# Attention and two gated feed-forward layers: in later batches VectorE's maxima and low parts stand behind an inverse

## The chip, the cores and the metric

One core of one Trainium2 chip runs the whole kernel. The metric is the device time of one execution in microseconds (us), less is better.

## What is computed

Attention over 4 batches of 8 heads, 576 positions, 64 columns a head; its output is one matrix of 2304 tokens x 512, which goes through two feed-forward layers. Heads 0 to 3 see a local window of 32 positions, heads 4 to 7 the positions at a distance that 32 divides.

```python
scores = scale * np.matmul(q, k.transpose(0, 1, 3, 2))
mask_local = (rel >= 0) & (rel < stride)          # stride = 32
mask_strided = (rel >= 0) & (pos[None, :] % stride == pos[:, None] % stride)
scores = np.where(masks[None, :, :, :], scores, -1000000000.0)
scores = scores - np.max(scores, axis=-1, keepdims=True)
attn = np.exp(scores)
attn = attn / (np.sum(attn, axis=-1, keepdims=True) + 1e-09)
out = np.matmul(attn, v)
x = out.transpose(0, 2, 1, 3).reshape(2304, 512)
xn = x / np.sqrt(np.mean(x * x, axis=-1, keepdims=True) + 1e-06) * rms_g
g = xn @ w_gate                                   # 512 x 1536
x = (g * (1.0 / (1.0 + np.exp(-g))) * (xn @ w_val)) @ w_out
```

The second layer is the last two lines again, with weights of its own and without the norm. All is float32.

## The kernel before

**Products.** A float32 matrix is held as a high part, rounded to the type that TensorE multiplies at full speed (fp32r), and a low part, what is left. A product is three matmuls: high by high, high by low, low by high. ScalarE casts the high part (L305 of a weight, L1000 of the tokens), VectorE subtracts it from the float32 source and so gets the low part (`lo`, L309, of a weight; L1001 in `split`, of the tokens). The gate's weights come by DMA into `raw` and `dh` buffers, are scaled (L288 and its neighbours), and split.

**Attention.** Each of the four batches has ten groups: five of strided heads and then five of local heads. A group goes through steps. `softmax_step` (L663): TensorE makes the scores in a PSUM bank; `top` has VectorE add the mask and take the negative maximum of each row, one instruction a head (L677, into `e` and `nb`; a program's listing shows a second row behind each, for the column `nb`); `exp` has ScalarE take the exponential and the row sums (L686); `norm` has VectorE add 1e-9 to the sums (L696) and take the inverse (L697, `rc`), and GpSimd multiply the weights by it (L703). `turn_step` (L712): TensorE transposes the weights into a bank (L80), and ScalarE (L87) or VectorE (L89) copies the bank to SBUF. A last step multiplies by V; its output is copied into `x` in SBUF and stored. Transposes of Q and K (`qn`, to `qT` and `kT`) go the same way, through L80 and L87 or L89. After the first batch five banks (a0, a1, y1, y2, y3) go round among these steps. A transpose or product that writes a bank has to wait until the bank's last reader is done.

**Feed-forward in between.** While attention runs, the first layer already works on the tokens that are ready, in segments of 256 or 512 tokens (the first at token 0, then 256, 512, 1024, 1536 and 1792). For each of twelve column blocks of 128 it makes the gate product (`gate`, bank `b_g`), the silu of it (L977, L978, `sg`), the value product (bank `b_v`), their product (L985), that one's high and low parts (L988 and L989, `hh` and `hl`), and the product with `w_out` (`down`). Between these, calls of `point()` let the attention steps go on by one phase: so TensorE's work alternates. The scheduler orders each engine's queue by a priority of each instruction; the feed-forward's own pieces have a higher one (`ahead`). After all attention, from about 206 us on, the remaining work is a long run of feed-forward passes that combine blocks so that seven products do for eight; these fill the rest of the span.

**Tokens.** `split` (L998) makes the high and low parts of a segment's tokens, for each of four column chunks. `here` (L1005) calls it for what attention has just left in SBUF. `split_x` (L1015) calls it for the columns that attention wrote to DRAM earlier: `load_x` has them loaded into `xraw`, two tiles, each with a single buffer that the next segment's load fills again. SyncE issues that load at L160.

**Order.** An instruction can be put behind another on the same engine without a wait: `tc.issue_after` sets an edge that only the order of issue keeps. The kernel uses it like this:

```python
    def behind(eng):
        return tc.issue_after(last[eng]) if eng in last else nullcontext()
```

`last["dve"]` and `last["act"]` hold VectorE's and ScalarE's latest `top`, `exp`, `silu` or `hidden` instruction, and `lo` stands behind `last["dve"]`. The functions that the diff touches follow, with the profile's line numbers.

Of the kernel before, what the change touches and what calls it, by code (L numbers as in the profile page):

```python
# [8 lines left out]
F32 = mybir.dt.float32  # L9
# [3 lines left out]
ALU = mybir.AluOpType  # L13
# [12 lines left out]
def attn_ffn_ffn(ctx: ExitStack, tc: tile.TileContext, q, k, v, w1g, w1v, w1o, rms_g, w2g, w2v, w2o, out):  # L26
    nc = tc.nc
# [65 lines left out]
    last = {}  # L93
# [211 lines left out]
            nc.scalar.copy(out=t[:, 0], in_=src)  # L305

    def lo(t, src):
        with behind("dve"):
            nc.vector.tensor_tensor(out=t[:, 1], in0=src, in1=t[:, 0].bitcast(F32), op=ALU.subtract)  # L309

    def weight_step(m, c, z, park=False):
# [11 lines left out]
        def second():  # L323
            lo(cell["t"], cell["h"])
            spent(cell["bk"], 4)
            wt[m, c, z] = cell["t"]
            wdone.add((m, c, z))
# [154 lines left out]
    def behind(eng):  # L482

        return tc.issue_after(last[eng]) if eng in last else nullcontext()
# [10 lines left out]
    class Attention:  # L495
# [167 lines left out]
        def softmax_step(self, ready, key, qn, kn, mks, mms):  # L663

            cell = {}
            nt = len(mks)

            def pe():
                cell["s"] = mms()

            def top():
                sp = cell["s"]
                cell["e"] = e = self.p2.tile([128, 4, 128], F32, tag="e", name="e", bufs=6)
                cell["nb"] = nb = self.p2.tile([128, 32], F32, tag="nb", name="nb", bufs=6)
                for i, mk in sorted(enumerate(mks), key=lambda im: im[0] % 2):

                    r = nc.vector.tensor_tensor_reduce(out=e[:qn, i, :kn], in0=sp[i], in1=mk[:qn, :kn], scale=-0.125,  # L677
                                                       scalar=3.0e38, op0=ALU.add, op1=ALU.min, accum_out=nb[:qn, i:i + 1])
                if state["start"]:
                    last["dve"] = ins_of(r)  # L680

            def exp():
                e, nb = cell["e"], cell["nb"]
                cell["sums"] = sums = self.p2.tile([128, 32], F32, tag="sums", name="sums", bufs=6)
                for i in range(nt):
                    r = nc.scalar.activation(out=e[:qn, i, :kn], in_=e[:qn, i, :kn], func=AF.Exp, bias=nb[:qn, i:i + 1],  # L686
                                             scale=-1.0, accum_out=sums[:qn, i:i + 1])
                if state["start"]:
                    last["act"] = ins_of(r)

            def norm():
                e, sums = cell["e"], cell["sums"]
                rc = self.p2.tile([128, 32], F32, tag="rc", name="rc", bufs=6)
                self.nnorm = getattr(self, "nnorm", -1) + 1
                eng = nc.gpsimd
                nc.vector.tensor_scalar(out=sums[:qn, :nt], in0=sums[:qn, :nt], scalar1=1e-9, scalar2=None, op0=ALU.add)  # L696
                nc.vector.reciprocal(out=rc[:qn, :nt], in_=sums[:qn, :nt])  # L697
                if eng is None:
                    for i in range(nt):
                        nc.vector.tensor_scalar(out=e[:qn, i, :kn], in0=e[:qn, i, :kn], scalar1=rc[:qn, i:i + 1], scalar2=None,  # L700
                                                op0=ALU.mult)
                if eng is not None:
                    eng.tensor_tensor(out=e[:qn, :nt, :kn], in0=e[:qn, :nt, :kn], in1=rc[:qn, :nt].unsqueeze(2).to_broadcast([qn, nt, kn]), op=ALU.mult)  # L703
                if key[1] == 0 or not 3:
                    self.st[key] = e

            def put():
                self.st[key] = cell["e"]

            return Step([pe, top, exp, norm] + ([wait] * (3 - 1) + [put] if 3 and key[1] else []), ready, kind="s")  # L710

        def turn_step(self, key, qn, kn, nt):  # L712
# [223 lines left out]
    def pieces(parts, t0, n):  # L936

        for a, w, d in parts:
            lo, hi = max(a, t0), min(a + w, t0 + n)
            if lo < hi:  # L940
                yield lo - t0, lo - a, hi - lo, d
# [28 lines left out]
    def ins_of(r):  # L970
        return getattr(r, "ins", r)
# [19 lines left out]
    def x_tiles(si):  # L991
        if si not in tiles_of:
            p, w = pools[si % 2]
            tiles_of[si] = [tuple(p.tile([128, w], F32R, tag=f"x{z}{c}", name="x" + z) for z in "hl") for c in range(KC)]
        return tiles_of[si]

    @ahead
    def split(si, o, w, src):  # L998
        for c, (xh, xl) in enumerate(x_tiles(si)):
            ra = nc.scalar.copy(out=xh[:, o:o + w], in_=src(c))  # L1000
            rd = nc.vector.tensor_tensor(out=xl[:, o:o + w], in0=src(c), in1=xh[:, o:o + w].bitcast(F32), op=ALU.subtract)  # L1001
            if si == 0:
                last["act"], last["dve"] = ins_of(ra), ins_of(rd)

    def here(b, o, w):  # L1005

        lo, hi = b * S + o, b * S + o + w
        for si in range(1, min(cur[0] + 2, NA)):
            t0, n = segs[si][1:3]
            a, e = max(lo, t0), min(hi, t0 + n)  # L1010
            if a < e:
                have_to.setdefault(si, set()).add((lo, hi))
                split(si, a - t0, e - a, lambda c: att.x[b, c // 2][:, c % 2, a - b * S:e - b * S])

    def split_x(si):  # L1015
        t0, n = segs[si][1:3]
        if si in xraw:
            x0, x1, todo = xraw.pop(si)
            for lo, hi in todo:
                a, e = max(lo, t0), min(hi, t0 + n)  # L1020
                split(si, a - t0, e - a, lambda c: (x0, x1)[c // 2][:, c % 2, a - t0:e - t0])
        return tiles_of[si]
# [122 lines left out]
    with tc.high_priority(offset=PRIO_R):  # L1145
        split(0, 0, early[0][1], lambda c: att.x[0, c // 2][:, c % 2, :early[0][1]])
        xs_of = {0: tiles_of[0]}
# [443 lines left out]
    for n, (m, cs, t0) in enumerate(work):  # L1591
# [88 lines left out]
        c = chunks[-1]  # L1680
# [47 lines left out]
```

## Time and profile before

| | |
|---|---|
| three runs | 993.5, 998.85, 996.44 us (median 996.44) |
| the profiled execution | 994.36 us |
| its span | 992.5 us, 17794 instructions |
| mean granted TensorE clock | 0.997 of full speed |
| TensorE busy | 968.8 us, 98% of the span |
| VectorE busy | 578.1 us, 58% |
| ScalarE busy | 577.9 us, 58% |
| GpSimd busy | 388.1 us, 39% |

The time of an execution is the span, from its first to its last instruction, and 1.9 us around it (994.36 - 992.5). The profile was taken of one execution, so its rows add up to its span and not to the median. The granted clock is that of TensorE: 1.00 is 2.4 GHz, and the lower of its two levels, 1.2 GHz, reads as 0.50; a mean between them is a stretch that has both. "Idle before" in brackets is the time in which the engine did nothing just before an instruction, with what ended it; "issue" there means that the profile shows nothing that it waited for.

### The profile page before, as it was taken

The page shows a single profiled execution, that of the slowest core. Times are in us where ns is not written, and L with a number is a line of the kernel's source. Part 1 is how long each engine was busy: PE and PEld are TensorE (multiplying, and loading weights), DVE is VectorE, ACT ScalarE, POOL GpSimd, SP SyncE. Part 2 cuts the span into 40 slices and gives each one's busy share as a digit, 9 for nine tenths or more (in the row PEclk, how much of TensorE's full clock was granted, in tenths as well). Part 3 has the DMA queues.
Part 4 walks back from the last instruction along what each step waited for, and adds up shares of the span by engine and source line. Part 5 has one row for each costly group of instructions (what it writes and reads, how often), then busy time and mean ns, then how long its engine had stood idle before and what let it go on. Part 6 is the DMA issues. An engine that isn't in the chain of part 4 may idle for free.

```text
span 992.5 us, 17794 instructions
## 1 busy us (share of the span) xinstructions
PE 968.8 (98%) x6054; PEld 892.0 (90%) x6054; DVE 578.1 (58%) x1319; ACT 577.9 (58%) x1465; POOL 388.1 (39%) x416
## 2 busy tenths in 40 slices
PE   8889999999999999999999999999999999999998
PEld 8778877778989999999999998999999999989997
DVE  5786777856436556466656646545557554653334
ACT  6988686855545555556564546555666546553431
POOL 3221252641321637343534646471615344341500
PEclk9989999999999999999999999999999999999999
DMA  7884648829994756995759685466888396864311
GB/s 197 230 218 147 162 153 260 261 90 303 307 319 151 219 173 224 323 321 174 251 175 325 220 279 209 155 221 241 310 269 267 114 342 220 289 206 161 97 53 64
DMA packets 168455, 215.89 MB, mean 218 GB/s; under 512 B 46860, under 2 KB 122028, under 8 KB 168364
## 3 DMA queue, kind: packets, MB, share of 16 engines
q1 hardware_dynamic: 158559, 199.48, 62.4%
q10 hardware_dynamic: 9805, 15.27, 4.3%
q8 instruction: 48, 0.79, 0.3%
q14 instruction: 43, 0.35, 0.1%
HBM read 142.87 MB, written 71.83 MB: 216 GB/s over the span
## 4 chain that ended last, share of the span: by engine, by line
PE 84%; ACT 6%; DMA 5%; DVE 3%; issue 1%; POOL 1%; SPq 0%; DVEq 0%; POOLq 0%; ACTq 0%
PE b_y L76 36%; PE b_a L76 17%; PE b_g L76 14%; PE b_v L76 13%; PE b_y L80 2%; ACT e L686 2%; DMA raw<-in_moe_w_out_dram 1%; PE b_a L80 1%; DMA pk<-dh 1%; ACT raw L288 1%; PE b_v L72 1%; ACT dh L280 1%; DMA pk<-raw 1%; DVE dh L297 1%; DMA ob<-part 1%
## 5 line engine op out<-in xcount | busy, mean ns | idle before, releaser
L1401 POOL TENSOR_TENSOR xl<-xst,xh 128x384 fp32r<-128x384 f32 x196 | 211.8, 1102 | 178.9 <-ACT xh L1400 60.1
L76 PE MATMUL b_y<-xh,w 128*128 128x384 f32 (+1 forms) x800 | 215.6, 335 | 1.4 <-ACT t L1458 1.1
L76 PEld LDWEIGHTS b_y<-xh,w 128*128 128x128 f32 x800 | 145.9, 188 | 4.4 <-ACT t L1458 1.7
L76 PE MATMUL b_a<-xh,w 128*128 128x384 f32 (+2 forms) x512 | 141.3, 335 | 1.8 <-ACT t L1458 1.6
L76 PE MATMUL b_y<-xl,w 128*128 128x384 f32 (+1 forms) x400 | 133.8, 334 | 0.0
L76 PE MATMUL b_g<-xh,w 128*128 128x384 f32 (+2 forms) x408 | 125.6, 348 | 0.1
L76 PE MATMUL b_v<-xh,w 128*128 128x384 f32 (+2 forms) x344 | 104.6, 347 | 1.4 <-ACT t L1472 1.4
L76 PEld LDWEIGHTS b_a<-xh,w 128*128 128x128 f32 x512 | 93.2, 188 | 5.4 <-ACT t L1458 3.1
L386 POOL TENSOR_TENSOR raw<-dh 128x256 f32<-128x256 f32 x40 | 29.6, 758 | 160.6 <-DVE dh L297 69.0
L1400 ACT CAST xh<-xst 128x384 fp32r<-128x384 f32 x196 | 91.5, 520 | 0.0
L76 PE MATMUL b_a<-xl,w 128*128 128x384 f32 (+2 forms) x256 | 85.8, 335 | 0.0
L76 PE MATMUL b_y<-hh,w 128*128 128x384 f32 (+2 forms) x304 | 81.2, 341 | 0.0
L76 PEld LDWEIGHTS b_g<-xh,w 128*128 128x128 f32 x408 | 75.6, 190 | 5.5 <-issue 0.5
L76 PEld LDWEIGHTS b_y<-xl,w 128*128 128x128 f32 x400 | 75.2, 188 | 1.8
L76 PE MATMUL b_g<-xl,w 128*128 128x384 f32 (+2 forms) x204 | 69.1, 339 | 0.0
L76 PEld LDWEIGHTS b_v<-xh,w 128*128 128x128 f32 x344 | 62.9, 188 | 6.5 <-ACT t L1472 1.7
L703 POOL TENSOR_TENSOR e<-e,rc 128x384 f32<-128x384 f32 (+3 forms) x40 | 37.0, 929 | 79.3 <-DVE nb L677 17.0
L76 PE MATMUL b_y<-w,hh 128*128 128x512 f32 x216 | 67.1, 391 | 0.0
L686 ACT ACTIVATE e<-e,nb 128x96 f32<-128x96 f32 (+2 forms) x152 | 56.7, 377 | 5.0 <-DVE nb L677 5.0
L76 PE MATMUL b_v<-xl,w 128*128 128x384 f32 (+2 forms) x172 | 58.0, 337 | 0.0
L76 PEld LDWEIGHTS b_y<-hh,w 128*128 128x128 f32 x304 | 54.8, 188 | 3.1 <-issue 0.2
L1478 DVE TENSOR_TENSOR b_y<-b_y,t 128x384 f32<-128x384 f32 x56 | 31.7, 566 | 41.7 <-ACT b_y L1472 40.8
(216 smaller groups left out, 2150.8 us busy)
## 6 DMA issues: line engine op xcount, KB each, us to landing
w<-pk SPq DMA_DIRECT2D x48, 512.0 KB
raw<-in_moe_w_gate_dram SPq DMA_DIRECT2D x24, 512.0 KB
raw<-in_moe_w_val_dram SPq DMA_DIRECT2D x24, 512.0 KB
raw<-in_moe_w_out_dram SPq DMA_DIRECT2D x24, 512.0 KB
pk<-raw ACTq DMA_DIRECT2D x48, 256.0 KB
part<-ob SPq DMA_DIRECT2D x48, 256.0 KB
xst<-y_d SPq DMA_DIRECT2D x30, 384.0 KB
xst<-xq SPq DMA_DIRECT2D x28, 384.0 KB
```

What stands on the lines that cost most here:

```text
L72: traced(nc.tensor.matmul(att.fill, att.warm[:, :128], att.warm, start=True, stop=True))
L76: traced(nc.tensor.matmul(out_, a, b_, start=start, stop=stop, **how))
L80: traced(nc.tensor.transpose(out_, a, one))
L280: nc.scalar.activation(out=cell["h"], in_=cell["hw"].bitcast(F32), func=AF.Copy, scale=2.0 ** -112)
L288: nc.scalar.activation(out=cell["r"], in_=cell["lw"], func=AF.Copy, scale=LOW)
L297: nc.vector.scalar_tensor_tensor(out=h, in0=h, scalar=3, in1=cell["r"], op0=ALU.logical_shift_left, op1=ALU.bitwise_or)
L386: paced(nc.gpsimd.tensor_tensor(out=t[:, z], in0=a, in1=b, op=ALU.subtract))
L686: r = nc.scalar.activation(out=e[:qn, i, :kn], in_=e[:qn, i, :kn], func=AF.Exp, bias=nb[:qn, i:i + 1], scale=-1.0, accum_out=sums[:qn, i:i ...
L703: eng.tensor_tensor(out=e[:qn, :nt, :kn], in0=e[:qn, :nt, :kn], in1=rc[:qn, :nt].unsqueeze(2).to_broadcast([qn, nt, kn]), op=ALU.mult)
L1400: nc.scalar.copy(out=xh[:, kk], in_=src[:, kk])
L1401: paced(nc.gpsimd.tensor_tensor(out=xl[:, kk], in0=src[:, kk], in1=xh[:, kk].bitcast(F32), op=ALU.subtract), ("pe", None))
L1478: nc.vector.tensor_tensor(out=s, in0=s, in1=v, op=ALU.mult)
```

## The change

Every inverse of row sums that `norm` makes is noted as `last["sum"]`, if the second part of the group's key is not 0; that is so in batches 1 to 3 and not in batch 0. Three kinds of VectorE instructions then stand behind the inverse noted last: the maxima of `top`, the low parts of weights in `lo`, and the low parts of tokens in `split`. "Noted last" goes by the order in which the program is written down: whatever is written after an inverse comes behind it in VectorE's queue. No instruction is added or taken away, and none changes its size. Until the first inverse of batch 1 is noted, nothing is different.

```diff
--- before.py
+++ after.py
@@ -305,7 +305,7 @@
             nc.scalar.copy(out=t[:, 0], in_=src)
 
     def lo(t, src):
-        with behind("dve"):
+        with behind("dve"), behind("sum"):
             nc.vector.tensor_tensor(out=t[:, 1], in0=src, in1=t[:, 0].bitcast(F32), op=ALU.subtract)
 
     def weight_step(m, c, z, park=False):
@@ -674,8 +674,9 @@
                 cell["nb"] = nb = self.p2.tile([128, 32], F32, tag="nb", name="nb", bufs=6)
                 for i, mk in sorted(enumerate(mks), key=lambda im: im[0] % 2):
 
-                    r = nc.vector.tensor_tensor_reduce(out=e[:qn, i, :kn], in0=sp[i], in1=mk[:qn, :kn], scale=-0.125,
-                                                       scalar=3.0e38, op0=ALU.add, op1=ALU.min, accum_out=nb[:qn, i:i + 1])
+                    with behind("sum"):
+                        r = nc.vector.tensor_tensor_reduce(out=e[:qn, i, :kn], in0=sp[i], in1=mk[:qn, :kn], scale=-0.125,
+                                                           scalar=3.0e38, op0=ALU.add, op1=ALU.min, accum_out=nb[:qn, i:i + 1])
                 if state["start"]:
                     last["dve"] = ins_of(r)
 
@@ -694,7 +695,9 @@
                 self.nnorm = getattr(self, "nnorm", -1) + 1
                 eng = nc.gpsimd
                 nc.vector.tensor_scalar(out=sums[:qn, :nt], in0=sums[:qn, :nt], scalar1=1e-9, scalar2=None, op0=ALU.add)
-                nc.vector.reciprocal(out=rc[:qn, :nt], in_=sums[:qn, :nt])
+                r = nc.vector.reciprocal(out=rc[:qn, :nt], in_=sums[:qn, :nt])
+                if key[1]:
+                    last["sum"] = ins_of(r)
                 if eng is None:
                     for i in range(nt):
                         nc.vector.tensor_scalar(out=e[:qn, i, :kn], in0=e[:qn, i, :kn], scalar1=rc[:qn, i:i + 1], scalar2=None,
@@ -998,7 +1001,8 @@
     def split(si, o, w, src):
         for c, (xh, xl) in enumerate(x_tiles(si)):
             ra = nc.scalar.copy(out=xh[:, o:o + w], in_=src(c))
-            rd = nc.vector.tensor_tensor(out=xl[:, o:o + w], in0=src(c), in1=xh[:, o:o + w].bitcast(F32), op=ALU.subtract)
+            with behind("sum"):
+                rd = nc.vector.tensor_tensor(out=xl[:, o:o + w], in0=src(c), in1=xh[:, o:o + w].bitcast(F32), op=ALU.subtract)
             if si == 0:
                 last["act"], last["dve"] = ins_of(ra), ins_of(rd)
```

The lines of the changed kernel stand 1 to 4 further down: the maxima are L678, the addition L697, the inverse L698, the low parts of tokens L1005, the `sg` product L988, `hl` L992, the cast of tokens L1003.

What this does to the engines' orders is seen in three places. TensorE's order is the same in both programs.

**Batch 1, VectorE, from the addition to the sums of the first group** (`sums` of 126 rows; the L677 rows are the maxima of a later group, from banks y3 and a0; `w` are weights, `xl` and `sg` pieces of the feed-forward). Before:

```order
L696 TENSOR_SCALAR sums_1083<-sums_1083 126x4
L677 ISA e_1117,nb_1118<-b_y3_1094,ms_100 108x108
L677 ISA nb_1118 108x1
...
L677 ISA e_1117,nb_1118<-b_a0_1095,ms_100 108x108
L677 ISA nb_1118 108x1
L309 TENSOR_TENSOR w1_2_0_989<-dh_951,w1_2_0_989 128x512
L309 TENSOR_TENSOR w1_2_1_1009<-dh_962,w1_2_1_1009 128x512
L1001 TENSOR_TENSOR xl_1068<-x00_791,xh_1067 128x256
L978 SCALAR_TENSOR_TENSOR sg_1058<-sg_1058,b_g_1004 128x256
L1001 TENSOR_TENSOR xl_1070<-x00_791,xh_1069 128x256
L697 RECIPROCAL rc_1108<-sums_1083 126x4
```

Now:

```order
L697 TENSOR_SCALAR sums_1083<-sums_1083 126x4
L309 TENSOR_TENSOR w1_2_0_989<-dh_951,w1_2_0_989 128x512
L309 TENSOR_TENSOR w1_2_1_1009<-dh_962,w1_2_1_1009 128x512
L1005 TENSOR_TENSOR xl_1068<-x00_791,xh_1067 128x256
L981 SCALAR_TENSOR_TENSOR sg_1058<-sg_1058,b_g_1004 128x256
L1005 TENSOR_TENSOR xl_1070<-x00_791,xh_1069 128x256
L698 RECIPROCAL rc_1108<-sums_1083 126x4
L678 ISA e_1117,nb_1118<-b_y3_1094,ms_100 108x108
```

The four maxima have moved from ahead of the inverse to behind it; the two weights, the two token low parts and the `sg` product are still ahead.

**Batch 2, VectorE, the low parts of the third segment's first 64 tokens, which come from `xraw`.** Before, the first of them stood nearly a hundred rows further up:

```order
L978 SCALAR_TENSOR_TENSOR sg_1435<-sg_1435,b_g_1386 128x256
L1001 TENSOR_TENSOR xl_1850<-xraw_1766,xh_1849 128x64
L309 TENSOR_TENSOR w1_3_2_1390<-dh_1315,w1_3_2_1390 128x512
L985 SCALAR_TENSOR_TENSOR sg_1435<-sg_1435,b_v_1450 128x256
L1001 TENSOR_TENSOR xl_1852<-xraw_1766,xh_1851 128x64
L1001 TENSOR_TENSOR xl_1854<-xraw_1768,xh_1853 128x64
```

Now they stand together, behind an inverse, the maxima of one more group and an `sg` product (the L678 rows left out are the like of the two shown):

```order
L697 TENSOR_SCALAR sums_2031<-sums_2031 126x4
L698 RECIPROCAL rc_2056<-sums_2031 126x4
L678 ISA e_2065,nb_2066<-b_a1_2042,ms_100 108x108
...
L678 ISA e_2065,nb_2066<-b_y1_2043,ms_100 108x108
L678 ISA nb_2066 108x1
L988 SCALAR_TENSOR_TENSOR sg_1976<-sg_1976,b_v_1993 128x256
L1005 TENSOR_TENSOR xl_1850<-xraw_1766,xh_1849 128x64
L1005 TENSOR_TENSOR xl_1852<-xraw_1766,xh_1851 128x64
L1005 TENSOR_TENSOR xl_1854<-xraw_1768,xh_1853 128x64
L1005 TENSOR_TENSOR xl_1856<-xraw_1768,xh_1855 128x64
```

The load that fills `xraw` next, in SyncE's queue, now also waits for VectorE to have read it here; before, these reads lay far ahead of it.

**Batch 3, VectorE and ScalarE, at the first gate of the fourth segment** (`xl_2741` to `xl_2747` are its tokens' low parts; `xraw_3441` and `xraw_3443` are the next segment's load). VectorE now (before, the four low parts stood far above, and the last inverse shown here right ahead of `hl`, behind the maxima):

```order
L697 TENSOR_SCALAR sums_2950<-sums_2950 108x4
L698 RECIPROCAL rc_2963<-sums_2945 108x4
L698 RECIPROCAL rc_2967<-sums_2950 108x4
L678 ISA e_3006,nb_3007<-b_y3_2994,ms_100 108x108
...
L992 TENSOR_TENSOR hl_3000<-sg_2934,hh_2999 128x512
L1005 TENSOR_TENSOR xl_2741<-xraw_2535,xh_2740 128x128
L1005 TENSOR_TENSOR xl_2743<-xraw_2535,xh_2742 128x128
L1005 TENSOR_TENSOR xl_2745<-xraw_2537,xh_2744 128x128
L1005 TENSOR_TENSOR xl_2747<-xraw_2537,xh_2746 128x128
L434 TENSOR_TENSOR dh_2824<-dh_2824 128x256
```

ScalarE before:

```order
L87 COPY x31_3067<-b_a1_3054 128x18x6 x2
L87 COPY kT30_3087<-b_y2_3079 128x512
L977 ACTIVATE sg_3100<-b_g_3028 128x512
L427 CAST raw_2723<-raw_2721 128x512
L87 COPY qT30_3071<-b_y3_3090 128x512
L1000 CAST xh_3586<-xraw_3441 128x192
L1000 CAST xh_3588<-xraw_3441 128x192
L87 COPY kT30_3087<-b_a0_3095 128x512
```

ScalarE now:

```order
L87 COPY x31_3067<-b_a1_3054 128x18x6 x2
L1003 CAST xh_3586<-xraw_3441 128x192
L87 COPY kT30_3087<-b_y2_3079 128x512
L1003 CAST xh_3588<-xraw_3441 128x192
L980 ACTIVATE sg_3100<-b_g_3028 128x512
L427 CAST raw_2723<-raw_2721 128x512
L1003 CAST xh_3590<-xraw_3443 128x192
L1003 CAST xh_3592<-xraw_3443 128x192
L87 COPY qT30_3071<-b_y3_3090 128x512
```

The low parts come late, behind `hl`; and the four casts of the next `xraw` stand ahead of the copy that empties bank y3. That load, too, now waits for VectorE's late reads of the buffer it fills.

## Rows read from the trace of the kernel before

**Rows 1.** the page of the whole span: part 1, then part 4 (chain)

```profile
PE 968.8 (98%) x6054; PEld 892.0 (90%) x6054; DVE 578.1 (58%) x1319; ACT 577.9 (58%) x1465; POOL 388.1 (39%) x416
...
PE 84%; ACT 6%; DMA 5%; DVE 3%; issue 1%; POOL 1%; SPq 0%; DVEq 0%; POOLq 0%; ACTq 0%
```

**Rows 2.** windows: stretch, its us, engines' busy us (x), PEclk, DMA share, GB/s

```profile
64.00:72.00 8.00, 7.69 (x40) 6.73 (x41) 4.50 (x20) 6.06 (x24) 3.02 (x4) 0.57 0.89 269
...
210.00:992.50 782.50, 773.50 (x4218) 729.70 (x4216) 426.75 (x719) 410.87 (x887) 316.81 (x318) 1.00 0.67 223
```

**Rows 3.** waits of TensorE, 60 to 210 us: total us, times, longest

```profile
PE b_a L80 <- issue: 2.5, 1, 2.5
PE b_y L80 <- POOL e L703: 2.1, 1, 2.1
```

**Rows 4.** timeline of VectorE near 60 us (start, us, engine, line, operation; [idle])

```profile
59.55 0.26 DVE L677 CUSTOM_DVE_ANT_0 e<-b_y,ms 108x108 f32<-108x108 f32 x1
...
60.30 1.28 DVE L309 TENSOR_TENSOR w<-dh,w 128x512 fp32r<-128x512 f32 x2
...
62.51 0.16 DVE L697 RECIPROCAL rc<-sums 126x4 f32<-126x4 f32 x1
```

**Rows 5.** timelines of GpSimd and TensorE near 63 us

```profile
62.85 1.41 POOL L703 TENSOR_TENSOR e<-e,rc 126x504 f32<-126x504 f32 x1 [9.70 <-DVE nb L677]
...
64.31 0.65 PE L80 MATMUL b_y<-ident,e 126*126 126x126 f32 x4 [2.15 <-POOL e L703]
```

**Rows 6.** timelines of ScalarE, VectorE and TensorE, 67 to 80 us: a weight

```profile
67.41 0.70 ACT L288 ACTIVATE raw<-raw 128x512 uint32<-128x512 uint32 x1 [1.00 <-DMA raw<-in_moe_w_gate_dram]
...
76.89 1.15 ACT L305 CAST w<-dh 128x512 fp32r<-128x512 f32 x2
...
78.65 0.68 DVE L309 TENSOR_TENSOR w<-dh,w 128x512 fp32r<-128x512 f32 x1
...
79.39 0.39 PE L76 MATMUL b_g<-xh,w 128*128 128x256 f32 x1
```

**Rows 7.** timelines of TensorE, VectorE and ScalarE, 118 to 131 us (batch 2)

```profile
118.78 0.39 PE L76 MATMUL b_g<-xl,w 128*128 128x512 f32 x1
...
119.58 0.41 DVE L985 SCALAR_TENSOR_TENSOR sg<-sg,b_v 128x256 f32<-128x256 f32 x1
...
122.65 0.50 ACT L1000 CAST xh<-xraw 128x128 fp32r<-128x128 f32 x2 [0.48 <-DMA xraw<-x_d]
...
122.98 1.61 DVE L1001 TENSOR_TENSOR xl<-xraw,xh 128x128 fp32r<-128x128 f32 x4
...
130.20 0.20 DVE L89 COPY x<-b_a 128x36 f32<-128x36 f32 x1
...
130.50 0.31 PE L80 MATMUL b_a<-ident,qn 64*128 64x64 f32 x2 [2.47 <-issue]
```

**Rows 8.** timelines of five engines, 179 to 187 us (batch 3)

```profile
179.40 0.39 PE L76 MATMUL b_g<-xl,w 128*128 128x512 f32 x1
...
179.55 0.17 DVE L697 RECIPROCAL rc<-sums 108x4 f32<-108x4 f32 x1
...
179.64 1.11 DVE L989 TENSOR_TENSOR hl<-sg,hh 128x512 fp32r<-128x512 f32 x1
...
180.15 1.36 POOL L703 TENSOR_TENSOR e<-e,rc 108x432 f32<-108x432 f32 x1
...
181.48 2.70 POOL L1211 TENSOR_TENSOR xst<-xst 128x384 f32<-128x384 f32 x2
...
182.34 1.03 SPq L160 DMA_DIRECT2D xraw<-x_d  x2
...
184.76 0.59 ACT L87 COPY qT<-b_y 128x512 f32<-128x512 f32 x1
...
186.35 0.35 ACT L1000 CAST xh<-xraw 128x192 fp32r<-128x192 f32 x1 [1.00 <-DMA xraw<-x_d]
...
186.79 0.58 PE L80 MATMUL b_y<-ident,e 108*108 108x108 f32 x4
```

## The prediction, made before the changed kernel ran

> **What bounds the kernel now.** I read the page first: TensorE is busy in 98% of the span and holds 84% of the chain that ended last [rows 1]. So a change of VectorE's order can only be worth what TensorE idles because of VectorE, or what it will newly idle. From 210 us to the end TensorE is busy for 773.5 of 782.5 us [rows 2], and the diff moves nothing there; what is won or lost before is carried to the end one for one. The place to look is the three batches of attention after the first, 56 to 206 us. The list of TensorE's waits from 60 to 210 us has two of more than 2 us [rows 3]: 2.1 us for the normalised weights (the GpSimd multiply, L703), in batch 1, and 2.5 us that the profile calls "issue", in batch 2. The timeline says what the second is: the transpose at 130.50 writes bank a1, and VectorE's copy out of that bank (L89) starts at 130.20 and ends at 130.40 [rows 7]. After the first the granted clock averages 0.57 from 64 to 72 us [rows 2], that is mostly the lower level, 1.2 GHz: 8.00 x 0.43 = 3.4 us more. After the second it did not fall.
>
> **Batch 1, the gain.** The inverse of the first group's sums starts at 62.51, GpSimd multiplies from 62.85 to 64.26, and the transpose starts at 64.31 [rows 4, 5]. In VectorE's order the four maxima of a later group, 59.55 to 60.30, stood ahead of that inverse [rows 4]; now they stand behind it. Everything else ahead of it stays, so the inverse comes 0.75 us earlier, and the 2.1 us of waiting become 1.4. The clock I leave as it is. How much of a gain can survive? The third matmul of the gate at 79.39 needs the low part of a weight, made at 78.65 from a cast that ScalarE starts at 76.89 (two casts in 1.15 us, so this one ends near 77.47). That weight's load has ScalarE waiting until 67.41 [rows 6], and nothing here makes the load earlier. With the low part (0.68) right behind the cast the matmul could start at 78.15, so a cap of 79.39 - 78.15 = 1.2 us lies on all that batch 1 can win. Term: **-0.75 us**; bounds 0 (later maxima hold up the next steps) and -1.2.
>
> **Batch 2, a late low part.** The first gate of the third token segment multiplies with `xl` at 118.78, with no wait [rows 7]: the 64 columns that come from DRAM had long been split. Now these four subtractions stand behind the second group's inverse, the maxima of a further group and the `sg` product. In the row that product starts at 119.58 and takes 0.41 [rows 7]; the same work stands ahead of it as before, so the first low part is done near 120.3, and with 0.3 for the subtraction TensorE gets it near 120.6: a new wait of 1.8 us. But 10 us later TensorE idles for 2.47 us anyway [rows 7], and the new wait only eats from that, if VectorE's copy at 130.20 stays in place. Two things move that copy. The next `xraw` load now waits until these subtractions have read the old contents of its buffer (near 121), and the casts that waited for it at 122.65 stand ahead of a copy of the transposed weights on ScalarE: 0.6 us later. Against it, the four low parts that took 1.61 us at 122.98 leave this stretch [rows 7], but the copy behind them waits for TensorE's transposes anyway. Term: **+0.4 us**; bounds -1.6 (those low parts' time is won in full) and +1.8 (nothing is absorbed).
>
> **Batch 3, the same with less cover.** The fourth segment's first gate needs `xl` at 179.40 [rows 8]. The low parts now come behind the last inverse (179.55 before), which changes places with four maxima, so VectorE comes to `hl` near 179.9 (0.2 later than in the row, for the inverse and the gaps between); that took 1.11 us [rows 8]: 181.0. The first low part at 1.61 / 4 = 0.4 [rows 7] ends at 181.4, a wait of 2.0 us. A second path says the same. The next `xraw` load was issued at 182.34, and the cast waited for it until 186.35 [rows 8], 4.0 us. It now waits for the second low part, 181.8, so it lands near 185.8. The four casts of `xraw` now stand ahead of the copy that frees bank y3, which ran at 184.76 [rows 8]: 185.8 plus the pieces ahead of the copy (a kT copy, a `sg` activation, a weight cast at some 0.5 each, four casts at 0.25) gives 188.3, and its end 188.9. The transpose at 186.79 writes that bank [rows 8]; it comes 2.1 us later. The two are in series, so the later one counts. Behind it TensorE has no wait to give back. Term: **+2.0 us**; bounds 0 (the chains find slack) and +4.0 (the load lands 2 us later still).
>
> The other exchanges, an inverse ahead of one or two maxima of the local groups, I cost at nothing: their transposes follow microseconds later, and TensorE has matmuls queued ahead of them, and no other line of its list of waits reaches 2 us [rows 3]. Without that cover each would cost at most the 0.17 us of an inverse [rows 8].
>
> **Sum.** -0.75 + 0.4 + 2.0 = +1.65 us. The profiled execution took 994.36 us, so 996.0; the median of the runs shown is 996.44, and on it the forecast is **998.1 us**, +0.17%. A measurement of this kernel can tell about 0.5% (5 us) from no change, so this is no change.
>
> **A rule against the change.** In the rows, `hl` began at 179.64, while GpSimd was at work, and ended at 180.75, although the next GpSimd multiply ran from 180.15 to 181.51 [rows 8]: slowed, not shut out. The Trainium skill, page "SBUF — State Buffer", section "Who interferes with whom", says that VectorE instructions with two SBUF inputs contend with GpSimd's reads, and that the shared port pair is an exclusive lock. If that lock were held for whole instructions, the low parts of batch 3 would wait for the end of GpSimd's run of work; the trace agrees on the contention and not on a full block.
>
> **Rivals.**
> *The clock stays up in batch 1.* With 1.4 us of idling in place of 2.1 the clock may not fall, and the 3.4 us return. For it: 2.47 us of idling in batch 2 took no clock. Against it: the cap of 1.2 us, since TensorE would run ahead only to wait for the weight. If the cap doesn't hold: -0.75 - 3.4 + 0.4 + 0 (with batch 3 at its lower bound) = -3.75, 992.7 us on the median. Chance 0.12.
> *The clock falls in batch 3 (slower).* The new waits at 179.40 and at the y3 bank are near each other; an idling of 2.1 us did bring the clock down in batch 1. It decides from there on: if TensorE idles 2.1 us or more in one piece near 180, another 3.4 us are due: +1.65 + 3.4 = +5.05, 1001.5 us. Against it: 2.47 us in batch 2 did not. Chance 0.15.
> *The low parts are shut out by GpSimd.* Batch 3's low parts come only after GpSimd's work: the multiply ends at 181.51, and two additions (2.70 us together) that begin near 181.5 end near 184.2 [rows 8]; 184.2 + 0.4 - 179.40 = 5.2 in place of 2.0: +4.85, 1001.3 us. [...] Chance 0.05.
> *The new waits are hidden.* Both batches stay at 0: -0.75, 995.7 us, no change either. Chance 0.13.
>
> **How the numbers follow.** The forecast has 0.55. Between 992.5 (the clock rival) and 1002.0 (batch 3 with a fall of the clock) lie the forecast, the hidden waits, and most of both clock rivals; left out are batch 2 and 3 at their upper bounds with a fall of the clock. Faster by over 0.5% would need more than the whole clock loss of batch 1: 0.05. Slower by over 0.5% is half of the two slower rivals and the sums of upper bounds: 0.15. The rest, 0.80, is within 0.5%.
>
> **What would show it.** Right: the inverse of batch 1 near 61.8 and the wait for L703 near 1.4 us; TensorE waiting some 1.8 us for VectorE's `xl` (L1005) near 119 and 2 us near 179.5; the wait near 128 shorter than 2.47 us; the copy out of y3 behind casts that wait for a load; from 210 us the same busy TensorE, shifted by 1 to 2 us. Wrong: no wait at the two gates (the low parts come in time), a clock of 1.0 all through 60 to 75 us with the gate at 79.39 several us earlier (the cap fails), or a fall of the clock near 120 or 180 us.

## The result and the profile after

The changed kernel takes **1001.71 us** in the median of 7 runs (999.65 to 1004.82), the kernel before 994.86 us in 7 runs on the same chip (991.5 to 998.85). The ratio is **1.0066, 95% interval 1.0045 to 1.0088**: slower by 6.6 us (6.9 between the medians), small, but clear of the noise. Forecast were 998.1 us and a range of 992.5 to 1002.0. The time lies in the range and on the side of the sum (+1.65 us), but four times as far out, where the rival of a falling clock in batch 3 stood (1001.5), and beyond the 0.5% that was given a chance of 0.80. That it lies in the range is luck in part: the forecast stood on the median of three runs of the kernel before, 996.44 us, and seven runs give 994.86. On that base the range would end at 1000.4.

Each time below was taken together with runs of the kernel before on the same chip, and each ratio is to those; their medians are 993.2 to 994.7 us.

The profiled execution has a span of 999.5 us where that of before had 992.5. The page of the changed kernel, parts 1 and 4 [rows 1]:

```profile
PE 969.9 (97%) x6054; PEld 892.1 (89%) x6054; DVE 579.8 (58%) x1319; ACT 577.4 (58%) x1465; POOL 385.8 (39%) x416
...
PE 83%; ACT 6%; DMA 5%; DVE 4%; issue 1%; POOL 0%; SPq 0%; ACTq 0%; DVEq 0%; POOLq 0%
```

The counts in this row are the same as before, and no engine's busy time differs by more than 2.3 us. The windows of the changed kernel (columns as in [rows 2]: behind the stretch come its length, the five engines' busy times, the granted clock, DMA share and GB/s):

```profile
64.00:72.00 8.00, 6.51 (x55) 5.57 (x54) 5.21 (x30) 5.55 (x23) 2.84 (x3) 1.00 0.97 313
160.00:170.00 10.00, 8.14 (x44) 6.89 (x45) 8.76 (x17) 5.48 (x12) 2.57 (x5) 0.83 0.79 231
180.00:190.00 10.00, 6.69 (x32) 4.91 (x33) 8.75 (x26) 4.11 (x15) 7.08 (x8) 0.67 0.58 187
217.00:999.50 782.50, 773.16 (x4218) 729.79 (x4216) 428.59 (x719) 410.80 (x887) 315.89 (x318) 1.00 0.67 223
```

The last row against that of before (773.50 us busy in a stretch of the same length) shows that the 7.0 us are complete by 217 us. The clock no longer falls in batch 1 (1.00 for 0.57), and falls in two other places. TensorE's waits, the longest first (total us, times, longest) [rows 3]:

```profile
PE b_g L76 <- DVE xl L1005: 4.8, 2, 3.3
PE b_y L76 <- DVE dg L879: 1.9, 2, 1.6
PE b_a L80 <- issue: 1.3, 1, 1.3
PE b_g L76 <- DVE w L309: 1.3, 1, 1.3
PE b_y L80 <- POOL e L706: 1.0, 1, 1.0
PE b_y L80 <- DVE nb L678: 0.8, 1, 0.8
```

TensorE's order is the same in both kernels, so the start of one and the same matmul can be compared in the two timelines:

| matmul | before | after | shift |
|---|---|---|---|
| last one ahead of the wait in batch 1 | 61.88 | 61.91 | +0.03 |
| transpose of the first group | 64.31 | 63.19 | -1.12 |
| third matmul of the gate (weight) | 79.39 | 79.36 | -0.03 |
| gate of the third segment, `xl` | 118.78 | 120.37 | +1.59 |
| transpose into bank a1 | 130.50 | 131.06 | +0.56 |
| first product with `dg` | 160.97 | 161.56 | +0.59 |
| transpose behind it, `qn` 108*64 | 167.11 | 169.28 | +2.17 |
| gate of the fourth segment, `xl` | 179.40 | 185.05 | +5.65 |
| transpose into bank y3 | 186.79 | 194.38 | +7.59 |
| transpose of the next group | 192.77 | 199.81 | +7.04 |

So in these two profiles batch 1 gave nothing, batch 2 cost 0.56, a lower clock from 163 us on 1.6, the wait in batch 3 3.5 (5.65 - 2.17), a lower clock behind it 1.9, and 0.55 came back. In a second profile of each kernel (both are reported below) the last matmul of the table starts at 199.67 and 193.56: 6.1 us.

The timelines around the two gates of that kernel, TensorE first, then VectorE and GpSimd of batch 3:

```profile
120.37 0.50 PE L76 MATMUL b_g<-xl,w 128*128 128x512 f32 x1 [1.45 <-DVE xl L1005]
...
131.06 0.31 PE L80 MATMUL b_a<-ident,qn 64*128 64x64 f32 x2 [1.29 <-issue]
...
185.05 0.80 PE L76 MATMUL b_g<-xl,w 128*128 128x512 f32 x1 [3.31 <-DVE xl L1005]
```

```profile
182.22 1.77 DVE L992 TENSOR_TENSOR hl<-sg,hh 128x512 fp32r<-128x512 f32 x1
183.91 2.49 DVE L1005 TENSOR_TENSOR xl<-xraw,xh 128x128 fp32r<-128x128 f32 x4
```

```profile
181.67 1.77 POOL L706 TENSOR_TENSOR e<-e,rc 108x432 f32<-108x432 f32 x2 [0.41 <-DVE rc L698]
183.40 2.65 POOL L1215 TENSOR_TENSOR xst<-xst 128x384 f32<-128x384 f32 x2
```

`hl` took 1.77 us where [rows 8] had 1.11, and the low parts begin while GpSimd works with hardly a pause (0.08 us between the two additions).

### The profile page after: what moved, and what is told of

The parts are those of the page before. It is cut to its first block, busy times and chain, and to the rows that moved or that the text cites. A ratio compares the mean times of both kernels' runs of the same rounds, so it can differ in the third digit from the quotient of the medians.

```text
span 999.5 us, 17790 instructions
## 1 busy us (share of the span) xinstructions
PE 969.9 (97%) x6054; PEld 892.1 (89%) x6054; DVE 579.8 (58%) x1319; ACT 577.4 (58%) x1465; POOL 385.8 (39%) x416
## 4 chain that ended last, share of the span: by engine, by line
PE 83%; ACT 6%; DMA 5%; DVE 4%; issue 1%; POOL 0%; SPq 0%; ACTq 0%; DVEq 0%; POOLq 0%
PE b_y L76 35%; PE b_a L76 18%; PE b_g L76 15%; PE b_v L76 13%; ACT e L687 2%; PE b_y L80 2%; DMA pk<-raw 1%; DMA pk<-dh 1%; PE b_a L80 1%; ACT dh L280 1%; ACT raw L288 1%; DMA ob<-part 1%; DMA kn<-in_k_dram 1%; DMA raw<-in_moe_w_out_dram 1%; DMA raw<-in_moe_w_val_dram 1%
## 5 line engine op out<-in xcount | busy, mean ns | idle before, releaser
L706 POOL TENSOR_TENSOR e<-e,rc 128x384 f32<-128x384 f32 (+3 forms) x40 | 35.7, 895 | 86.1 <-DVE nb L678 23.4
```

## The experiments

My first theory after this: the whole loss comes from the late low parts of tokens, and the maxima are harmless. The rival: maxima that come later hold up what is behind them. The part of the change in `lo` has no share: with or without it, alone or beside the rest, the programs of all engines are the same, instruction for instruction. The runs with the maxima or the tokens alone leave it out too.

**The maxima alone.**

```diff
-            with behind("sum"):
-                rd = nc.vector.tensor_tensor(out=xl[:, o:o + w], ...
+            rd = nc.vector.tensor_tensor(out=xl[:, o:o + w], ...
```

> The change without its part in split (low parts of tokens stay where they were) and without its part in lo, which by itself leaves every engine's order as it was; the maxima alone stand behind the inverse. Theory 1 (all of the loss comes from the late low parts of tokens, and the maxima win nothing because a weight holds the gate at 79.39): ratio to before 1.000, 994 to 996 us; TensorE has no wait for xl near 119 and 180, the wait for L703 in batch 1 is near 1.0 us in place of 2.1, the clock stays at 1.00 from 64 to 72 us, and the gate that came at 79.39 still comes at 79.4. Theory 2 (maxima that come later hold up the exponentials and copies behind them): ratio at least 1.004, 999 us or more, with new waits for nb, qT or kT.

Measured: 997.66 us in 12 runs, ratio 1.0034 (1.0011 to 1.0056). Theory 1 fails: the maxima bring about half of the loss. Its profile had the 1.0 us wait and the clock of 1.00 in batch 1, but TensorE's wait for the weight of L309 is 1.30 us here too. The profiled execution took 993.99 us, one of the fastest of the twelve, so it shows the waits but not the whole loss.

**The tokens alone.**

```diff
-                    with behind("sum"):
-                        r = nc.vector.tensor_tensor_reduce(...
+                    r = nc.vector.tensor_tensor_reduce(...
```

> The opposite half: only the low parts of tokens stand behind the inverse, the maxima stay where they were. Theory 1: as slow as the whole change, ratio 1.005 to 1.008; waits for xl of about 1.5 us near 120 and 2.5 to 3.5 us near 183, a lower clock behind the second, and in batch 1 the old wait of 2.1 us with its low clock. Theory 2: ratio 1.000 to 1.002.

Measured: 998.11 us in 12 runs, ratio 1.0027 (1.0007 to 1.0047), about the other half; waits for `xl` of 3.5 us in two, the longer 2.2, with a lower clock behind it (0.85 from 180 to 190 us). This profile, too, is of a fast execution (993.47 us). In it the clock did not fall in batch 1 although the wait there was the old one, 2.16 us. That made the mechanism of the maxima visible. ScalarE of the changed kernel, from the weight's load to the scaling (L280) of the next one, the first and last of two groups' exponentials between:

```profile
67.74 0.66 ACT L288 ACTIVATE raw<-raw 128x512 uint32<-128x512 uint32 x1 [2.27 <-DMA raw<-in_moe_w_gate_dram]
...
69.94 0.37 ACT L687 ACTIVATE e<-e,nb 108x108 f32<-108x108 f32 x1
...
71.09 0.37 ACT L687 ACTIVATE e<-e,nb 108x108 f32<-108x108 f32 x1
...
72.19 0.37 ACT L687 ACTIVATE e<-e,nb 108x108 f32<-108x108 f32 x1
...
72.85 0.68 ACT L280 ACTIVATE dh<-raw 128x512 f32<-128x512 f32 x1
```

The same of the run with the tokens alone, where one group's four exponentials stand there:

```profile
67.30 0.68 ACT L288 ACTIVATE raw<-raw 128x512 uint32<-128x512 uint32 x1 [0.71 <-DMA raw<-in_moe_w_gate_dram]
...
69.50 0.37 ACT L686 ACTIVATE e<-e,nb 108x108 f32<-108x108 f32 x1
...
70.99 0.68 ACT L280 ACTIVATE dh<-raw 128x512 f32<-128x512 f32 x1
```

From load to scaling it is 5.11 us in the one and 3.69 in the other: with the maxima moved, ScalarE idles longer until the load lands (2.27 us for 0.71), and a second group's exponentials, 4 x 0.37 us, then stand right in front of the weight.

In the kernel before this way is longer than either, 5.50 us, from 67.41 [rows 6]:

```profile
72.91 0.67 ACT L280 ACTIVATE dh<-raw 128x512 f32<-128x512 f32 x1
```

There the clock was low. Over all profiles of kernels whose wait in batch 1 was not filled, it is 5.11 to 5.13 us in each of the seven with the maxima of batch 1 moved; with the old order it is 3.69 to 3.71 in the three in which the clock stayed up behind the wait, and 5.50 and 5.47 in the two in which it fell.

**The whole without the fourth segment's tokens.**

```diff
-            with behind("sum"):
+            with behind("sum") if si != 3 else nullcontext():
```

> The whole change, but the low parts of the fourth segment's tokens (the ones needed near 180 us) are not put behind the inverse. Theory 1: the 3.3 us of waiting near 182 and the low clock behind it go, the wait of 1.4 us near 119 stays: +0.6 us, ratio 1.0005, and 1.002 if the clock falls near 163 as it did in the changed kernel's profile. Theory 2: as the whole change, 1.006.

Measured: 997.22 us in 12 runs, ratio 1.0030 (1.0010 to 1.0049). The 3.3 us of waiting are gone, and with them half of the loss: between the two theories, as the halves would have it. In its profile (997.25 us) the clock fell twice all the same, behind the wait for the weight (0.79 from 78 to 86 us) and near 190 us (0.83 from 184 to 194).

**The wait filled.** 26 matmuls into a free bank between the gate's first matmul and the one that waits.

```diff
+                    for _ in range(26):
+                        with tc.issue_after(ins_of(r)):
+                            traced(r := nc.tensor.matmul(fill[0][:, :256], att.warm[:, :128], att.warm, start=True, stop=True))
```

> The whole change, with 26 idle matmuls of 256 columns into a bank that is free, put into TensorE's order right where it waits for the low part near 182 us (they take about 3.0 us, less than the 3.3 us of the wait). If the lower clock behind the wait has its cause in the idling, the low part comes as late as in the changed kernel, the clock stays at 1.00 from 183 to 191 us, and the time falls by the 2.4 us that it cost there: 999 us, ratio 1.004. If the clock has no share in it (what follows waits for other things anyway): the same time as the whole change, 1.0066.

TensorE's timeline and the window:

```profile
182.19 3.28 PE L1037 MATMUL b_v<-warm 128*128 128x256 f32 x26
185.69 0.50 PE L76 MATMUL b_g<-xl,w 128*128 128x512 f32 x1 [0.22 <-DVE xl L1005]
```

```profile
180.00:190.00 10.00, 9.78 (x72) 8.24 (x71) 9.44 (x26) 5.03 (x20) 7.08 (x9) 1.00 0.64 204
```

The low part comes as late as before (185.69, in a profile that was 0.62 us later by the transpose of `qn` 108*64), and the clock stays at 1.00. That fits the idling as what brought it down, in one profile; in the run with GpSimd quiet below, the clock stayed up behind 2.38 us of idling here. The time did not fall, a miss: 1003.1 us in 6 runs, ratio 1.0072 (1.0047 to 1.0097), where 1.004 was expected. The profile lost as much elsewhere, to a clock that fell at 78 and at 416 us.

**The maxima by batch.** The parts in `lo` and `split` are left out here.

```diff
-                    with behind("sum"):
+                    with behind("sum") if key[1] == 1 else nullcontext():
```

> The maxima stand behind the inverse in batch 1 only; nothing else of the change. Theory A (the moved maxima push the exponentials of two groups in front of ScalarE's work on the weight, so its low part comes at 78.6 and the gate at 79.4, whatever the clock does, while the order of before reaches 77.1 in executions in which the clock stays up): TensorE waits 1.3 us for w of L309 near 79, four exponentials stand ahead of the scaling (L280) near 73, ratio 1.001 to 1.0025. Theory B (batch 1 is harmless, the loss of the maxima comes from batches 2 and 3): ratio 1.000.

and with `key[1] > 1`:

> The maxima stand behind the inverse in batches 2 and 3 only. Theory A: ratio 1.000 to 1.0015; the idling near 130 us some 0.3 us longer, and 0.7 us lost near 185, as in the run with all the maxima. Theory B: ratio 1.003, as with all the maxima.

Measured: batch 1 alone 998.09 us in 12 runs, ratio 1.0025 (1.0003 to 1.0047); batches 2 and 3 alone 998.25 us in 12, ratio 1.0030 (1.0011 to 1.0050). Both parts cost; the times can't tell which costs more. In the profile of the second, TensorE's idling near 130 is 3.30 us for 2.47, and the one near 185 1.28 for 0.43; with all maxima they were 2.75 and 1.28. Behind the first the clock fell (0.66 from 130 to 140 us). The profile of batch 1 alone took 992.73 us, the fastest of its twelve runs: what the slower ones lost is not seen in it.

**GpSimd quiet.** The additions of the second block's first half are left out, and with them a part of the computation.

```diff
-                paced(nc.gpsimd.tensor_tensor(out=f[z, kk], in0=f[a, kk], in1=f[b, kk], op=op))
+                if not t0 or kk:
+                    paced(nc.gpsimd.tensor_tensor(out=f[z, kk], in0=f[a, kk], in1=f[b, kk], op=op))
```

> The whole change, but GpSimd leaves out the four additions of the second block of 768 tokens, first half of the columns, of which two run from 183.4 to 186.1 us in the changed kernel (so this part of the computation is left out). If the low parts of tokens took up to 1.09 us there in place of 0.28 because GpSimd works on SBUF at the same time, then hl beside GpSimd's multiplies stays at 1.5 to 1.8 us, the first low part falls from 1.09 to 0.3 and TensorE's wait for it from 3.3 to 2.5 us. If GpSimd has no share in it, both stay.

VectorE's low parts of tokens (ns: least, median, most) in the changed kernel, in this run, and in the run with the tokens alone:

```profile
L1005 DVE TENSOR_TENSOR xl<-xraw,xh x4: 277/677/1087, 183.9 to 186.1; 128x128 fp32r<-128x128 f32 x4
```

```profile
L1005 DVE TENSOR_TENSOR xl<-xraw,xh x4: 277/279/989, 183.0 to 184.3; 128x128 fp32r<-128x128 f32 x4
```

```profile
L1004 DVE TENSOR_TENSOR xl<-xraw,xh x4: 278/1076/1092, 178.8 to 181.0; 128x128 fp32r<-128x128 f32 x4
```

One and the same instruction takes 0.28 us, or 1.08 beside GpSimd. In the changed kernel it is the first and the third that take 1.08 and 1.09, one for each addition, and both end 0.15 us behind the end of an addition (184.84 and 186.05). With the additions gone the third takes 0.28 like the second and the fourth. The first still took 0.99: it ended 0.15 us behind GpSimd's second multiply, which ran until 183.84. TensorE's wait is 2.38 us, near the 2.5 expected, but not for the reason expected: `hl`, forecast at 1.5 to 1.8 us, took 0.90, and the first low part, forecast at 0.3, did not. `hl` and GpSimd's multiplies in this run, then in the changed kernel:

```profile
181.62 2.22 POOL L706 TENSOR_TENSOR e<-e,rc 108x432 f32<-108x432 f32 x2 [0.41 <-DVE rc L698]
182.18 0.90 DVE L992 TENSOR_TENSOR hl<-sg,hh 128x512 fp32r<-128x512 f32 x1
```

```profile
182.22 1.77 DVE L992 TENSOR_TENSOR hl<-sg,hh 128x512 fp32r<-128x512 f32 x1
182.54 0.91 POOL L706 TENSOR_TENSOR e<-e,rc 108x432 f32<-108x432 f32 x1
```

In both, `hl` stands 0.31 to 0.32 us ahead of the second multiply. Here it came in between the two, and that multiply took 1.35 us; in the changed kernel the multiply took its 0.91 and `hl` ended 0.5 us behind it. Why one and not the other goes first is not settled. One run, 995.95 us.

**The kernel before, its wait in batch 1 filled.**

```diff
+                if key == ("s", 1, 0, 0):
+                    for _ in range(14):
+                        traced(nc.tensor.matmul(tp[:, :256], self.warm[:, :128], self.warm, start=True, stop=True))
```

> The kernel before, with 14 idle matmuls of 256 columns (1.7 us) in TensorE's wait of 2.1 us for the first group's normalised weights in batch 1. If the fall of the clock there costs the kernel before some 2.3 us to the end (the run with the tokens alone, in which it did not fall, had the gate of 79.39 at 77.12), and it falls in most executions: clock 1.00 from 64 to 72, the gate near 77.1, ratio 0.998. If the weight's low part holds the gate anyway, as I had it in the cap: no change, 1.000.

Measured: 1000.7 us in 8 runs, ratio 1.0060 (1.0039 to 1.0081), a miss on the wrong side. Batch 1 went as expected (clock 1.00, gate at 77.83 in a profile that was 0.75 us late ahead of the wait), but the clock fell near 130, and between 400 and 500 us TensorE waited twice, where ScalarE waits until a weight's buffer is stored. TensorE's and ScalarE's timelines:

```profile
411.48 0.44 PE L76 MATMUL b_v<-xh,w 128*128 128x384 f32 x1 [3.04 <-ACT t L1475]
```

```profile
410.39 0.66 ACT L280 ACTIVATE dh<-raw 128x512 f32<-128x512 f32 x1 [3.92 <-DMA pk<-dh]
```

In the kernel before that wait was 1.35 us. The filled kernel was run once more:

> The kernel before with the 14 idle matmuls in batch 1 once more, since it lost 6 us where 2 were to be won. Its first profile won the 2.5 us by 80 us, lost 2.8 us to a lower clock near 130, and 6.7 us between 400 and 500 us, where TensorE waited twice for 3.1 us behind a store that freed a weight's buffer. If those long waits belong to this kernel, they come back, with a time near 1000 us, ratio 1.006; if the first profile and its eight runs met them by chance, the waits near 410 and 460 are 1 us each and the ratio is 0.998 to 1.000.

Measured: 1001.21 us in 9 runs, ratio 1.0055 (1.0031 to 1.0078). The long waits are back (2.4 and 2.5 us, a lower clock behind each), and so is the fall near 130. Neither is this kernel's alone. The kernel before, run again below, waits 2.59 us at the first of these places, with a lower clock behind it (0.83 from 410 to 420 us), and the clock also fell near 130 in the profiles of the late tokens, of the changed kernel again and of the maxima in batches 2 and 3. The two waits together take 4.9 to 6.1 us in the three profiles with filled waits, and at most 3.5 us in the ten others of whole kernels. Why the stores land later there is not settled.

**One reorder that might have won.**

```diff
+                        last["rest"] = ins_of(nc.vector.tensor_copy(out=out_, in_=turned_[:, w]))
...
+            with behind("rest") if si == 3 else nullcontext():
```

> The kernel before with one order alone: the four low parts of the fourth segment's DRAM tokens (1.61 us at 122.98) stand behind VectorE's copy of the last Q columns of batch 2 (near 131 us), not behind an inverse near 180. If they held up the copies out of bank a1, TensorE's idling of 2.47 us before 130.50 falls to about 1.3, as in the two runs with the tokens' part, and nothing waits for them near 180: 1.2 us won by 210 us, ratio 0.999. If the copies were late for another reason, the 2.47 us stay and the ratio is 1.000.

Measured: 994.11 us in 12 runs, ratio 1.0005 (0.9992 to 1.0019). The idling is unchanged (TensorE, then VectorE ahead of the copy):

```profile
130.81 0.31 PE L80 MATMUL b_a<-ident,qn 64*128 64x64 f32 x2 [2.47 <-issue]
```

```profile
127.02 1.55 DVE L292 SCALAR_TENSOR_TENSOR raw<-raw 128x512 uint32<-128x512 uint32 x1
128.68 1.30 DVE L297 SCALAR_TENSOR_TENSOR dh<-dh,raw 128x512 uint32<-128x512 uint32 x1
129.90 0.68 DVE L292 SCALAR_TENSOR_TENSOR raw<-raw 128x512 uint32<-128x512 uint32 x1
130.50 0.20 DVE L89 COPY x<-b_a 128x36 f32<-128x36 f32 x1
```

The low parts did not hold up the copy; three weight steps stand right ahead of it. That fits the shorter idling in the changed kernel as TensorE's own lateness.

**Both kernels again.**

> The changed kernel once more, for a second profile and twelve more times. What comes from the order of the queues must come back: a wait of 1.3 us for the weight at 79.4, 1.45 us for xl near 120, 3 to 3.3 us for xl near 183 with a lower clock behind it. What came by chance need not: the fall of the clock near 163. Ratio 1.005 to 1.008.

> The kernel before once more, for a second profile. If the fall of the clock behind the wait in batch 1 comes in every execution, it is there again from 64.8 to 71.7 and the gate is at 79.4; if it comes by chance, it may be missing, and then the gate is near 77.1 and the span some 2 us less. Ratio 1.000.

The changed kernel: 1000.42 us in 6 runs, ratio 1.0078 (1.0057 to 1.0100). TensorE's waits and the window of batch 3 in its second profile:

```profile
PE b_g L76 <- DVE xl L1005: 4.8, 2, 3.3
PE b_y L76 <- DVE dg L879: 1.9, 2, 1.6
PE b_g L76 <- DVE w L309: 1.3, 1, 1.3
PE b_a L80 <- issue: 1.3, 1, 1.3
```

```profile
180.00:190.00 10.00, 6.68 (x38) 5.02 (x37) 9.54 (x26) 4.74 (x19) 7.09 (x9) 0.85 0.54 173
```

The waits are the same to a tenth; the clock fell again behind the wait for `xl` and again near 163, but also near 132. The kernel before: 993.99 us in 10 runs, ratio 1.0012 (0.9997 to 1.0026); its clock did not fall in batch 1. The two spans, 996.8 and 995.3 us, differ by 1.5 us only, where the start of the last matmul of the table differs by 6.1: behind 210 us this profile of the kernel before has the long wait near 410 us, and that of the changed kernel has not. The clock of the kernel before:

```profile
64.00:72.00 8.00, 5.69 (x48) 4.81 (x47) 6.56 (x32) 6.11 (x25) 4.35 (x4) 1.00 0.91 281
```

So what the wait in batch 1 costs can be read over all profiles, from the last matmul ahead of it to the third matmul of the gate (start to start):

| order of the maxima in batch 1 | runs (clock behind the wait) | us | mean |
|---|---|---|---|
| as before | before (low), late tokens (low), before again, tokens alone, batches 2 and 3 | 17.51, 17.55, 16.26, 15.08, 14.90 | 16.26 |
| moved | changed kernel, again, maxima, without segment 4, wait filled, batch 1, GpSimd quiet | 17.45, 17.01, 16.61, 17.63, 16.47, 17.21, 17.41 | 17.11 |

With the maxima moved the clock did not fall behind the wait for L706 in any of the seven, and yet the gate comes 0.85 us later on average, each time behind a wait of 1.28 to 1.31 us for the weight. The old order's values spread too far for that mean to say much alone. Split by the clock they say more: 15.4 us in the three in which it stayed up, 17.5 in the two in which it fell, and 17.1 with the maxima moved. Around the new wait the clock fell in three of the seven (without segment 4, wait filled, GpSimd quiet): from 78 to 86 us it is 0.79, 0.57 and 0.79. From this matmul to the gate of the third segment it then takes 42.5 to 43.7 us, and 41.0 in the two profiles of the changed kernel. In the five with the old order it fell in none there.

## Why the prediction was right, and where not

**What bounds the kernel.** Right: in the first pair of profiles nothing changed from 217 us on, and every microsecond that TensorE lost before stayed to the end but for 0.55. The second pair shows that the rest of the span can differ by several us from one execution to the next.

**Batch 1, -0.75.** The inverse came 0.73 us earlier (61.78), as forecast; the wait fell to 1.0 us, more than forecast, since GpSimd's multiply also took 1.02 us for 1.41. The step that failed is the cap: "nothing here makes the load earlier" was true, but I took the chain behind the load as fixed, and set the cap at 1.2 us of gain. It is not fixed: with the old order and a clock that stays up it is 1.8 us shorter than in the profile that I read (3.69 for 5.50), and the gate came 2.4 us earlier (15.08 for 17.51), beyond the cap. The change lengthens that chain by 1.42 us (5.11 for 3.69), because the maxima decide when ScalarE's exponentials come. The rival of the clock that stays up came true in every profile with moved maxima and was worth only 0.4 us (17.1 for 17.5), for this reason. Measured over the profiles: +0.85 on average, +1.7 against the old order with the clock up and -0.4 against it with the clock down; the times of the run with batch 1 alone (1.0003 to 1.0047) say that it is a loss. My bound, "later maxima hold up the next steps", should not have ended at 0.

**Batch 2, +0.4.** Right in mechanism and size: a wait of 1.45 us (1.8 forecast) that eats from the idling before the transpose into a1, net +0.56. The exchanges of the other groups, which I cost at nothing, are not free: the maxima of batches 2 and 3 alone make the kernel slower (1.0011 to 1.0050), with 0.3 to 0.8 us more idling near 130 and 0.85 more near 185.

**Batch 3, +2.0.** The mechanism was right, the size off: 3.5 us. I took `hl` at 1.11 us and the first low part at 0.4 from rows; they took 1.77 and 1.08 (183.91 to 184.99). That is 1.3 us more, the difference between 2.0 and the measured wait of 3.31. The earlier inverses themselves brought it about: two in a row let GpSimd begin two multiplies at 181.67, beside `hl`, and two additions at 183.40, beside the low parts. With the tokens alone, where one multiply stands there, `hl` took 1.09 us and the wait was 2.2, near my 2.0. The second path, over the late load and the copy out of y3, did not count: the transpose into y3 shifted by 7.59 us, the one before it (185.03 to 192.61) by 7.58.

**The rule that I set aside.** I read [rows 8] as "slowed, not shut out". Read again, they fit a lock held for one instruction: `hl` ended at 180.75, and the multiply issued at 180.15 took 1.36 us where 0.91 is usual for its size, as if it had begun when `hl` was done. The 1.08 us of the first low part are its 0.28 plus a wait for the addition that ran. The Trainium skill, page "SBUF — State Buffer", section "SBUF: two separate sides", says that of a VectorE instruction with two SBUF inputs and a GpSimd instruction the one that starts first gets the shared port pair for the whole instruction; the trace agrees on the whole instruction, with 0.28 against 1.08 us. It does not settle which goes first: in both profiles of the changed kernel `hl` (1.77 and 1.76 us) waited for two multiplies in a row, though it stood ahead of the second. My rival took the lock too far (blocked to the end of all of GpSimd's work, 5.2 us), and my sum not far enough.

**The clock.** Its fall behind the wait in batch 3 was a rival with a chance of 0.15. It came in both profiles of the changed kernel and cost 1.9 us in the first; with TensorE kept busy it stayed away, in one profile. With less idling there it fell behind 2.2 us (the tokens alone) and not behind 2.38 (GpSimd quiet). The fall near 163 came in both, too, but it came in five of the fourteen profiles taken, three of them of other kernels, behind the same two waits for `dg`, some 1.9 us together: which of such waits brings it is not settled.

**The sum.** Waits: 0.85 + 0.56 + 3.5 - 0.55 = 4.4 us. The mean granted clock was 0.9939 over 13 runs of the changed kernel and 0.9958 over 89 of the one before; at some 1000 us that is up to 1.9 us more. Together 6.3, where the ratios give 6.6 and 7.8 us. This is an estimate: three of the terms come from one pair of profiles, and the 0.85 already holds falls of the clock in batch 1. My +1.65 was right in sign and four times too small. No version tried was faster than the kernel before.

## What to carry to other kernels

An instruction that is put back behind another takes its whole chain along: ask which engine gets the work next, and what it will then stand in front of. The gain from an earlier inverse was real and ended at the next shared engine. Take the duration of a VectorE instruction with two SBUF inputs from a row in which GpSimd is as busy as it will be in the new order, or bound it by both (here 0.28 and 1.08 us; an instruction can wait for more than one, as `hl` did). And do not read a kernel's loss from one profile: here executions of one kernel differ by 5 us and more, and several of the profiles are of its fastest.

## What was not expected of the hardware

- The same wait of 2.15 us in batch 1, with the same orders ahead of it, brought TensorE's clock from 2.4 to 1.2 GHz in two of five profiles and left it up in three.
- A clock that stays up need not win anything: a fall there costs the old order 2.1 us at the next gate (17.5 for 15.4), and the changed kernel, whose clock stayed up, reaches that gate hardly earlier (17.1), since ScalarE's chain is 5.1 us there for 3.7.
- Filling TensorE's idle time kept its clock up in place, but a kernel with 14 more matmuls at 63 us had long waits for stores at 410 and 460 us in both of its profiles. One of the two also came in a profile of the kernel before.
